# Attention with a two-layer network on one core: each half of the last output block is stored by one transfer with two pieces of 64 rows, from SyncE, in place of two transfers

## The chip, the core and the metric

The kernel runs on one core of one Trainium2 chip. Times are microseconds of device time of that core, from one execution of the whole program. The kernel before takes 636.6 us (median of 3 runs, 635.3 to 640.33). One further execution was profiled: its own time is 637.86 us, and its span, from the first to the last instruction of the profile, is 636.1 us.

## What is computed

Four sequences of 576 tokens go through attention with 8 heads of 64, whose scores get a bias from a small network on the relative position. The result, 2304 tokens by 512, goes through two matrix products with a squared ReLU between them. Everything is float32 for the reader of the output.

```python
def _attn_ref(q, k, v, w1, b1, w2):
    ...
    scores = scale * np.matmul(q, k.transpose(0, 1, 3, 2))
    ...
    scores = scores + bias.transpose(2, 0, 1)[None, :, :, :]
    ...
    return np.matmul(attn, v).astype(np.float32)

def _moe_ref(x, w_in, w_out):
    h = np.maximum(x @ w_in, 0.0)
    return (h * h @ w_out).astype(np.float32)

def reference(**kwargs):
    ...
    x = np.ascontiguousarray(attn_out.transpose(0, 2, 1, 3)).reshape(B * S, H * D)
    return _moe_ref(x=x, **moe_kwargs)
```

## The kernel before

**Tiling.** The four sequences are two pairs p. A sequence has four whole blocks of 128 tokens and a remainder of 64; the block c = 0 holds the remainders of both sequences of a pair, 64 tokens in the lower 64 partitions and 64 in the upper ones. So a pair has five blocks, and `order` lists all ten (k = 0 to 9). For each block and head, `qk`, `softmax_a`, `softmax_b`, `turn` and `pv` do the attention; `norm` and `turn_x` scale and transpose the block's result; then `g1(n)`, `square(n)`, `g2(n)` do the network in eight units of hidden columns each (n = 8 k + u), and `store(k, b)` writes the block to `out`. Float32 operands are split into pairs of float16 tiles, so each product is three matmuls.

**The last block.** The last block, k = 9, is the remainder block of the second pair. For it `g2` is "halved": the 512 output columns are computed as two halves of 256 columns (L865 to L875), each in its own PSUM tile `blk["o", d]`, so that the first half is finished one group of six matmuls ahead of the second. `store` (L882 to L898) then takes the halves d = 0 and d = 1 in turn: one scaling instruction moves a half from PSUM to an SBUF tile `o` of 128 x 256 (ScalarE at L889 for d = 0, VectorE at L887 for d = 1), and two transfers bring it to `out`, one for the 64 rows of each sequence (L895). The two pieces of a half lie 576 rows apart in `out`. SyncE issues three of the four transfers, ScalarE the last (d = 1, bb = 1). All transfers write rows of 256 float32, 1 KB each, at a pitch of 2 KB.

**What sets the order.** `PROGRAM` is one long string of words written by hand; each word takes the generator of that kind one step further (`next(live[word], None)`), so what stands between two `yield`s is recorded at one word. Every engine runs its own instructions in the order in which they were recorded. The word `ou:9.0` is the last block's store; it stands once ahead of the last step of `g2:79` and then at the end of the string. SyncE issues nearly all transfers of the kernel in this order and does no arithmetic; a transfer that waits holds back those behind it. The program ends when the last transfer has landed and all engines have come to the closing branch (L1014).

Of the kernel before, what the change touches and what calls it, by code (L numbers as in the profile page):

```python
# [16 lines left out]
B, H, S, D = 4, 8, 576, 64  # L17
DM, DFF = 512, 2048
# [179 lines left out]
)  # L198


# [1 line left out]
def tile_attention_moe(  # L202
# [11 lines left out]
    nc = tc.nc  # L214
# [55 lines left out]
    def zn(key, i):  # L270
        v = ENG[key]
        return v[min(i, len(v) - 1)]
# [606 lines left out]
    def store(k, b):  # L879
        blk = blks[k]  # L880
        p, c = blk["p"], blk["c"]
        if k == len(order) - 1 and not c:  # L882
            for d in range(2):
                r = slice(256 * d, 256 * d + 256)
                o = r_p.tile([128, 512], F32, tag="r", name="o")
                if d:
                    nc.vector.tensor_scalar(o[:, 0:256], blk["o", d][:, 0:256], blk["os"][:, 0:1], None, op0=ALU.mult)  # L887
                else:
                    nc.scalar.activation(out=o[:, 0:256], in_=blk["o", d][:, 0:256], func=AF.Copy,  # L889
                                         scale=blk["os"][:, 0:1])  # L890
                yield
                for bb in range(2):
                    r0 = (2 * p + bb) * S + 512
                    q = nc.scalar if d and bb else nc.sync
                    q.dma_start(out=out[r0:r0 + 64, r], in_=o[64 * bb:64 * bb + 64, 0:256])  # L895
                    if not d or not bb:
                        yield
            return  # L898
        o = r_p.tile([128, 512], F32, tag="r", name="o")
        if zn("oe", 2 * k + b) == "A":  # L900
            nc.scalar.activation(out=o, in_=blk["o", b], func=AF.Copy, scale=blk["os"][:, b:b + 1])
        else:
            nc.vector.tensor_scalar(o, blk["o", b], blk["os"][:, b:b + 1], None, op0=ALU.mult)
        yield
        if c:
            r0 = (2 * p + b) * S + 128 * (c - 1)
            nc.sync.dma_start(out=out[r0:r0 + 128, :], in_=o)
        else:
            for bb in range(2):
                r0 = (2 * p + bb) * S + 512  # L910
                nc.sync.dma_start(out=out[r0:r0 + 64, :], in_=o[64 * bb:64 * bb + 64, :])
                if bb == 0:
                    yield
# [104 lines left out]
```

## Time and profile before

| | |
|---|---|
| median of 3 runs | 636.6 us |
| the profiled execution's own time | 637.86 us |
| its span | 636.1 us |
| TensorE busy | 597.7 us (94%) |
| VectorE, GpSimd, ScalarE busy | 428.1, 385.4, 366.5 us |
| mean granted TensorE clock | 0.981 of full speed |
| transfers of the last block | 4 of 64 KB, 3 from SyncE and 1 from ScalarE |

TensorE works nearly without a break up to its last matmul; what follows it is a short end piece in which a scaling instruction, the transfers and the closing of the program come one after the other. The change lies wholly in that end piece. In the rows below, times of day are microseconds from the start of the span, SPq and ACTq are SyncE and ScalarE issuing transfers, and "DMA share" is the mean busy share of the 16 DMA engines.

### The profile page before, as it was taken

To read this page: it belongs to the slowest core of one execution; us is meant where nothing else is said; L and a number is where in the kernel's file an instruction comes from. 1 tells how busy PE (TensorE), PEld (TensorE's weight loads), DVE (VectorE), ACT (ScalarE), POOL (GpSimd) and SP (SyncE) were. 2 spreads that over 40 slices of the span, in tenths; PEclk is the share of its full clock that TensorE was granted. 3 is DMA by queue.
4 is the path that set the end of the run, shared out by engine and by line. 5 is a ranking of instruction groups with operands and counts; after the bars stand their busy time and mean duration, and the time that the engine had idled before them with its cause. 6 is when DMAs were issued, how large, how long until landed. Compare 5 with 4: busy or idle time off the path is not lost.

```text
span 636.1 us, 15958 instructions
## 1 busy us (share of the span) xinstructions
PE 597.7 (94%) x6296; PEld 402.7 (63%) x6296; DVE 428.1 (67%) x840; ACT 366.5 (58%) x779; POOL 385.4 (61%) x389
## 2 busy tenths in 40 slices
PE   5658998899999999999999999999999999999997
PEld 2124576475767467667657865767676686577576
DVE  7988999899669796787974663566456463613321
ACT  5559997687777465645567455746636574214020
POOL 5766499989767435866866647555665555523221
PEclk9669999899999999999999999999999999999999
DMA  8999987778979969799789969559955787623000
GB/s 291 325 285 284 286 237 253 244 188 203 191 183 185 220 159 170 184 226 221 177 164 219 165 131 186 139 115 196 186 136 122 158 169 144 140 34 72 18 34 18
DMA packets 204426, 112.19 MB, mean 176 GB/s; under 512 B 166848, under 2 KB 179392, under 8 KB 204352
## 3 DMA queue, kind: packets, MB, share of 16 engines
q1 hardware_dynamic: 204272, 111.12, 75.2%
q8 instruction: 49, 0.80, 0.5%
q14 instruction: 25, 0.20, 0.1%
q10 hardware_dynamic: 80, 0.07, 0.0%
HBM read 55.44 MB, written 15.61 MB: 112 GB/s over the span
## 4 chain that ended last, share of the span: by engine, by line
PE 51%; DMA 5%; DVE 5%; POOL 4%; issue 3%; ACT 2%; SPq 1%; POOLq 0%; DVEq 0%; ACTq 0%
PE hp L837 20%; PE o L872 19%; PE pv L757 5%; PE sc L637 5%; DMA at<-a 3%; DMA xt<-xh 2%; POOL a L712 2%; PE bp L542 1%; DVE s L656 1%; POOL g L857 1%; DVE g L280 1%; ACT s L669 1%; DMA stg<-vd 1%; DVE r L851 1%; ACT a L276 1%
## 5 line engine op out<-in xcount | busy, mean ns | idle before, releaser
L837 PE MATMUL hp<-xt,winH 128*128 128x256 f16 (+1 forms) x1280 | 193.3, 262 | 2.0 <-DVE r L851 1.1
L872 PE MATMUL o<-woutH,g 128*128 128x512 f16 (+1 forms) x608 | 186.4, 369 | 2.2 <-POOL g L857 1.6
L837 PE MATMUL hp<-xt,winL 128*128 128x256 f16 (+1 forms) x640 | 161.7, 262 | 0.0
L857 POOL TENSOR_TENSOR g<-r,g 128x512 f16<-128x512 f32 (+1 forms) x80 | 88.4, 1108 | 88.3 <-DVE g L280 81.5
L872 PEld LDWEIGHTS <-g 128*128 128x128 f16 x912 | 84.3, 98 | 90.5 <-issue 4.5
L712 POOL TENSOR_TENSOR a<-s,a 128x1024 f16<-128x1024 f32 (+1 forms) x64 | 133.1, 2079 | 0.0
L837 PEld LDWEIGHTS <-winH 128*128 128x128 f16 x1280 | 117.8, 98 | 20.6 <-DVE r L851 1.2
L656 DVE CUSTOM_DVE_ANT_0 s<-sc,bt 128x576 f32<-128x576 f32 x144 | 104.6, 749 | 35.7 <-PE sc L637 15.2
L851 DVE TENSOR_TENSOR r<-hp,r 128x512 f32<-128x512 f32 (+1 forms) x80 | 50.7, 634 | 105.6 <-ACT r L849 105.2
L872 PE MATMUL o<-woutL,g 128*128 128x512 f16 (+1 forms) x304 | 112.1, 369 | 0.0
L669 ACT ACTIVATE s<-s,nm 128x576 f32<-128x576 f32 x120 | 92.9, 774 | 6.6 <-ACT nm L667 0.4
L710 POOL TENSOR_TENSOR a<-s,a 128x128 f16<-128x128 f32 (+1 forms) x64 | 30.3, 473 | 105.6 <-ACT a L276 73.7
L849 ACT ACTIVATE r<-hp 128x512 f32<-128x512 f32 (+1 forms) x80 | 43.7, 546 | 85.4 <-PE hp L837 75.2
L757 PE MATMUL pv<-v,at 128*128 128x64 f16 (+5 forms) x2112 | 87.8, 203 | 1.9 <-ACT at L276 1.2
L667 ACT ACTIVATE nm<-mx,esc 128x1 f32<-128x1 f32 x120 | 34.4, 287 | 84.2 <-DVE mx L656 84.0
L276 ACT ACTIVATE a<-s 128x1152 f16<-128x1152 f32 (+1 forms) x64 | 70.3, 1098 | 14.6 <-DMA at<-a 13.5
L837 PEld LDWEIGHTS <-winL 128*128 128x128 f16 x640 | 62.6, 98 | 5.8
L757 PEld LDWEIGHTS <-at 128*128 128x128 f16 (+1 forms) x1792 | 55.0, 100 | 10.4 <-issue 3.6
L477 DVE TENSOR_SCALAR hg<-tab_t 128x464 f32<-128x464 f32 (+17 forms) x88 | 60.9, 723 | 0.7 <-PE bp L542 0.6
L280 DVE TENSOR_SCALAR g<-r 128x512 f16<-128x512 f32 (+1 forms) x64 | 48.0, 754 | 18.4 <-PE o L872 17.4
L637 PE MATMUL sc<-k,q 64*128 64x128 f16 (+1 forms) x768 | 58.2, 284 | 1.3 <-DVE mx L656 1.2
L637 PEld LDWEIGHTS <-q 64*128 64x128 f16 x768 | 39.6, 94 | 28.1 <-issue 19.0
(88 smaller groups left out, 687.1 us busy)
## 6 DMA issues: line engine op xcount, KB each, us to landing
bt<-biasd SPq DMA_DIRECT2D x64, 288.0 KB, 3.5
stg<-w_in SPq DMA_DIRECT2D x16, 512.0 KB, 6.0
stg<-w_out SPq DMA_DIRECT2D x16, 512.0 KB, 5.5
biasd<-be SPq DMA_DIRECT2D x16, 295.5 KB, 6.2
bt<-biasd SPq DMA_DIRECT2D x32, 144.0 KB, 4.7
qst<-qd SPq DMA_DIRECT2D x32, 128.0 KB, 3.3
out<-o SPq DMA_DIRECT2D x16, 256.0 KB, 2.5
v<-vd SPq DMA_DIRECT2D x8, 320.0 KB, 7.0
```

Of the source, the lines that this page charges most:

```text
L276: nc.scalar.activation(out=out, in_=in_, func=AF.Copy, scale=scale)
L280: nc.vector.tensor_scalar(out, in_, scale, None, op0=ALU.mult)
L477: nc.vector.tensor_scalar(ht, src, scl[:, n:n + 1], None, op0=ALU.min)
L637: i = nc.tensor.matmul(out=sc[:, o:o + w], lhsT=qt[r, qz, qs], rhs=kt[r, z, k0:k0 + w], start=(m == 0), stop=(m == 2), tile_position=(64 * ...
L656: nc.vector.tensor_tensor_reduce(s[:, 576 * b:576 * b + 576], sc[:, sb:sb + 576], bt, inv, 3.0e38, ALU.add, ALU.min, mx[:, b:b + 1])
L669: nc.scalar.activation(out=sl, in_=sl, func=AF.Exp, scale=-1.0, bias=mx[:, b:b + 1] if f32 else nm[:, b:b + 1], accum_out=su[:, h, b:b + 1])
L712: eng.tensor_tensor(av[:, :, 640:1152], ev[:, :, 0:512], av[:, :, 0:512], op=ALU.subtract)
L757: nc.tensor.matmul(out=dst, lhsT=lhsT, rhs=rhs, start=b not in [x[1] for x in seq[:j]], stop=b not in [x[1] for x in seq[j + 1:]], tile_po ...
L837: nc.tensor.matmul(out=hp[:, f * T:f * T + T].rearrange("p (b t) -> p b t", b=nb), lhsT=wt[:, k, c0:c0 + 128], rhs=xt[:, 0:nb, z * 4 + k, ...
L851: nc.vector.tensor_tensor(rr, hp[:, 0:2 * T], rr, op=ALU.mult)
L857: eng.tensor_tensor(g[:, 1, 0:2 * T], rr, g[:, 0, 0:2 * T], op=ALU.subtract)
L872: nc.tensor.matmul(out=blk["o", b][:, 0:256] if halved else blk["o", b], lhsT=g[:, z, c0:c0 + 128], rhs=wt[:, 2 * u + f, d], start=(u == 0 ...
```

## The change

In `store`, for the last block, the loop over the two sequences goes. One transfer from SyncE takes the whole tile `o[:, 0:256]` (128 partitions) to a destination that is written out as a pattern of three steps: 2 pieces a whole sequence apart, 64 rows in each, 256 elements in a row. ScalarE issues no transfer any more. The string loses two words, since the store has two steps fewer.

```diff
-    "ou:9.0 ou:9.0 ou:9.0 ou:9.0 ou:9.0 "
+    "ou:9.0 ou:9.0 ou:9.0 "
...
                 yield
-                for bb in range(2):
-                    r0 = (2 * p + bb) * S + 512
-                    q = nc.scalar if d and bb else nc.sync
-                    q.dma_start(out=out[r0:r0 + 64, r], in_=o[64 * bb:64 * bb + 64, 0:256])
-                    if not d or not bb:
-                        yield
+                dst = out[2 * p * S + 512:2 * p * S + 576, r]
+                dst = bass.AP(tensor=dst.tensor, offset=dst.offset, ap=[[S * DM, 2]] + [list(x) for x in dst.ap])
+                nc.sync.dma_start(out=dst, in_=o[:, 0:256])
+                if not d:
+                    yield
             return
```

At the very end of the program the instructions on SyncE are, before (the destination's shape stands behind the names; `o_9543` is the half d = 0, `o_9553` the half d = 1, `DVE_49` and `Activation_49` count finished instructions of VectorE and ScalarE, and the DMAHW names count landed transfers):

```order
L825 DMA_TRANSPOSE xt_9135<-xh_9126 128x8x128 [waits DMAHW3_49,DVE_49]
L907 DMA out<-o_9272 128x512 [waits DMAHW4_49,Activation_49]
L907 DMA out<-o_9356 128x512 [waits DMAHW5_49,Activation_49]
L895 DMA out<-o_9543 64x256 [waits Activation_49]
L895 DMA out<-o_9543 64x256 [waits DMAHW7_49]
L895 DMA out<-o_9553 64x256 [waits DMAHW1_49,DVE_49]
L1014 UNCONDITIONAL_BRANCH
```

And of the changed kernel, on SyncE at the same place (`o_9552` is now the half d = 1; all line numbers behind the edit are one lower):

```order
L825 DMA_TRANSPOSE xt_9135<-xh_9126 128x8x128 [waits DMAHW3_49,DVE_49]
L906 DMA out<-o_9272 128x512 [waits DMAHW4_49,Activation_49]
L906 DMA out<-o_9356 128x512 [waits DMAHW5_49,Activation_49]
L894 DMA out<-o_9543 2x64x256 [waits Activation_49]
L894 DMA out<-o_9552 2x64x256 [waits DMAHW7_49,DVE_49]
L1013 UNCONDITIONAL_BRANCH
```

Three transfers became two; the destination of both begins with a count of 2. The transfer of the second half stands directly behind that of the first and waits for VectorE's scaling and for the transfer of an earlier block. On ScalarE the end of the program before is:

```order
L849 ACTIVATE r_9409<-hp_9366 128x256 [waits DMAHW4_49,PE_49,Activation_49]
L849 ACTIVATE r_9489<-hp_9439 128x256 [waits PE_49,Pool_49]
L849 ACTIVATE r_9507<-hp_9464 128x256 [waits PE_49,Pool_49]
L889 ACTIVATE o_9543<-o0_9275,os_9115 128x256 [waits DMAHW5_49,PE_49,Activation_49]
L895 DMA out<-o_9553 64x256 [waits DVE_49]
L1014 UNCONDITIONAL_BRANCH
```

In the changed kernel the row `L895 DMA` is gone from ScalarE and the other rows stand as they did. On TensorE, VectorE and GpSimd no instruction is added, removed or moved.

## Rows read from the trace of the kernel before

**Rows 1.** Chain that ended last, 600:637 us: start us, us, what (first and last pieces)

```profile
599.11 1.16 POOL g L857
...
623.70 2.68 PE hp L837 x48
626.38 5.25 PE o L872 x48
631.63 0.02 issue
631.66 0.48 DVE o L887
```

**Rows 2.** Timeline, 624:637 us: start us, us, engine line op out<-in xcount [idle before]

```profile
631.05 0.47 ACT L889 ACTIVATE o<-o,os 128x256 f32<-128x256 f32 x1 [4.19 <-PE o L872]
631.35 0.27 PE L872 MATMUL o<-woutH,g 128*128 128x256 f16 x1
631.55 1.79 SPq L895 DMA_DIRECT2D out<-o  x3
631.66 0.48 DVE L887 TENSOR_SCALAR o<-o,os 128x256 f32<-128x256 f32 x1 [3.94 <-PE o L872]
632.18 0.56 ACTq L895 DMA_DIRECT2D out<-o  x1
```

**Rows 3.** Waits of SyncE, 620:637 us: engine line, us in total, times, longest

```profile
SPq L895 <- ACT o L889: 14.0, 1, 14.0
SPq L1014 <- DMA out<-o: 1.4, 1, 1.4
SPq L1014 <- PEq L1014: 0.9, 2, 0.7
```

**Rows 4.** Line 895: ns min/median/max of one issue, first and last start us; landing

```profile
L895 SPq DMA_DIRECT2D out<-o x3: 513/540/585, 631.6 to 632.8; - x3
L895 ACTq DMA_DIRECT2D out<-o x1: 562/562/562, 632.2 to 632.2; - x1
...
DMA to landing us min/median/max: 2.0/2.0/2.3
```

**Rows 5.** DMA queues, 631:637 us: packets, MB, share of 16 engines

```profile
q1 hardware_dynamic: 240, 0.20, 13.3%
q10 hardware_dynamic: 80, 0.07, 4.5%
```

**Rows 6.** Stretches of the end: length, five engines busy (x instructions), clock, DMA share, GB/s

```profile
632.40:632.60 0.20, 0.00 (x0) 0.00 (x0) 0.00 (x0) 0.00 (x0) 0.00 (x0) 1.00 0.00 0
632.60:632.80 0.20, 0.00 (x0) 0.00 (x0) 0.00 (x0) 0.00 (x0) 0.00 (x0) 1.00 0.19 51
632.60:633.20 0.60, 0.00 (x0) 0.00 (x0) 0.00 (x0) 0.00 (x0) 0.00 (x0) 1.00 0.44 109
634.20:634.40 0.20, 0.00 (x0) 0.00 (x0) 0.00 (x0) 0.00 (x0) 0.00 (x0) 1.00 0.63 149
634.40:634.60 0.20, 0.00 (x0) 0.00 (x0) 0.00 (x0) 0.00 (x0) 0.00 (x0) 1.00 0.01 0
```

**Rows 7.** DMA queues and issues, 617.5:620 us, where one whole-block store runs

```profile
q1 hardware_dynamic: 144, 0.26, 27.2%
issues: line engine op xcount, KB each, median us to landing
out<-o SPq DMA_DIRECT2D x1, 256.0 KB, 2.0
```

**Rows 8.** The page's DMA queues over the whole span: packets, MB, share of 16 engines

```profile
q1 hardware_dynamic: 204272, 111.12, 75.2%
```

**Rows 9.** Line 416, loads of 64 x 4 x 64: ns of one issue, landing

```profile
L416 SPq DMA_DIRECT2D qst<-qd x8: 601/613/749, 1.7 to 501.1; - x8
...
DMA to landing us min/median/max: 2.5/3.8/5.0
```

## Prediction

> **What bounds the kernel now.** I read the chain of waits first: from 599 us to the end it is TensorE, with only 1.16 us of GpSimd and then 0.48 us of VectorE that are not matmuls [rows 1]. The change touches no matmul, so the first 631.6 us stay as they are, and all that can move is the end piece from there to 636.1. The timeline gives it step by step [rows 2]. ScalarE scales the first half from 631.05 to 631.52; TensorE ends at 631.62; VectorE scales the second half from 631.66 to 632.14. SyncE issues from 631.55 to 633.34 three transfers one after the other, about 0.54 us each [rows 2, 4]; ScalarE issues the fourth at 632.18. SyncE's last issue starts at 632.8 and lands 2.0 us after its start, at 634.8; ScalarE's lands at 632.18 + 2.3 = 634.5 [rows 4]. So the last to land is the third of SyncE's queue. Behind it SyncE waits at the closing branch, 1.4 us for the transfer and 0.9 for TensorE's queue to close [rows 3], and the span ends.
>
> For the DMA engines the stretches show [rows 6]: nothing before 632.6, first rows on their way in 632.6 to 632.8 (I take 632.7, about 1.15 us after the first issue began at 631.55), and no more data after about 634.4. From the end of the data to the end of the span are 636.1 - 634.4 = 1.7 us, which I keep for all cases: landing, then closing.
>
> **What the change removes.** Two of four issues: 0.54 us on SyncE and 0.56 on ScalarE [rows 4]. With 16 engines at work on each transfer this would be a gain. VectorE is done at 632.14, SyncE's first issue ends at about 632.1, so the second half would be issued at 632.2 in place of 632.8, and its first rows would run at 632.2 + 1.15 = 633.3.
>
> **What it adds.** An issue with three steps in the destination. None to `out` is in the trace; the nearest are the loads with 64 x 4 x 64, 0.613 us against 0.54 [rows 9, 4], so +0.07 us, and nothing below zero since a pattern of more steps has no cheaper row. Only the first of the two would be on the path, and I price it at 0 to 0.1. The second lies beside the first transfer's data. Nothing is queued behind either but the closing branch.
>
> **What it moves: which DMA engines carry the rows.** This is the term that decides. Each transfer of 64 rows shows 80 packets: 64 rows and 16 closing packets, one for each engine; SyncE's three show 240, that is 3 x 80 [rows 5]. A store of 128 rows shows 144 = 128 + 16 [rows 7]. So a transfer whose outermost count is 64 or 128 on both sides is dealt out over all 16 engines in whole rows, 4 or 8 to each. The new transfer has 128 on the side it reads and 2 on the side it writes. The trace has no such transfer, so the cost has two bounds. If the rows are still dealt out over 16 engines, each carries 8. If the work is cut along the outermost count and the cut must fit both sides, only two equal parts are possible: two engines with 64 rows each, and the other 14 idle. I take the second, since what is seen of the dealing is always an equal cut of an outermost count that both sides share, and 2 is all that these two share.
>
> The Trainium skill, page "DMA: Bandwidth & Descriptors", section "Why a DMA increments its semaphore by 16 and not by 1", states this: the engine count is the largest number up to 16 that divides the slowest dimension of both patterns, and a transfer from SyncE or ScalarE uses the lowest-numbered engines. By that rule the count here is 2, and both transfers go to the same two. No run here shows it yet; the trace agrees for 64 and 128 rows (16 closings). At that page's rate of about 27 GiB/s for an engine, 64 KB would take an estimated 2.3 us, and the time by it would be about 639.4 us.
>
> **The price of one row on one engine.** Two rows of the trace bound it. The store of 128 rows of 2 KB keeps the engines busy for 27.2% of 2.5 us x 16 = 10.9 us, or 85 ns for 2 KB [rows 7]; half is 43 ns for 1 KB. The four transfers at the end take (13.3% + 4.5%) x 6 us x 16 = 17.1 us for 256 rows, 67 ns for 1 KB [rows 5]; the first of them alone, 0.44 x 0.6 x 16 = 4.2 us for 64 rows, 66 ns [rows 6]. Is 67 a matter of the short row? If a packet cost f + s per KB, 67 and 85 would give f = 49 ns; but over the whole span 204272 packets of 544 bytes on average took 0.752 x 636.1 x 16 / 204272 = 37 ns each [rows 8], less than f alone. So the 64-row stores are slow for another reason, and they differ from the 2 KB store in that they read 64 partitions with 16 engines, where it reads 128. Two engines that read from 128 partitions crowd each other less than either. I take 46 ns, just above half of the 2 KB row, and keep 67 as the other end.
>
> **The sum.** A transfer is 64 x 46 ns = 2.94 us on its two engines. The second half's rows are ready at 633.3, while the first's run until 632.7 + 2.94 = 635.6; they queue behind them on the same two engines. Data ends at 632.7 + 5.9 = 638.6, and the span at 638.6 + 1.7 = 640.3, which is 4.2 us over 636.1. The profiled execution's 637.86 us would become 642.1; it stood 1.3 us above the median of 636.6, so for the median I expect 636.6 + 4.2 = 640.8 us, 0.66% more. A measurement of this kernel can tell about 1% from no change, so this is a small loss that counts as "within 1%".
>
> **Rivals.**
> Slow rows on two engines (slower by over 1%). The rows cost 67 ns as in the four transfers of before: 64 x 67 ns = 4.3 us a transfer, data until 641.3, span 643.0, +6.9, 643.5 us. For it: it is the price of just these 1 KB rows to just this place in memory [rows 5]. Against it: the 37 ns of the mean packet [rows 8], and that 16 engines no longer share 64 partitions. It decides from +6.4 us on, that is 8.1 us of data, 63 ns a row.
>
> Sixteen engines (a small gain). The pattern is dealt out over all engines: 8 rows each, 8 x 46 ns = 0.37 us; the second half runs from 633.3 to 633.7, span 635.4, -0.7, 635.9 us. For it: every transfer of the trace does so [rows 5, 7]; against it: the common count of 2. The Trainium skill, page "SBUF — State Buffer", section "Can I just issue two DMAs to hit both halves?", speaks for the change: two transfers of 64 partitions each reach only half the ports, one over 128 reaches all. The slow rows at the end (67 ns against 43) agree with it; what it would give here is this rival's time.
>
> Two engines each, but not the same two. The second half runs from 633.3 to 636.2 beside the first: span 637.9, +1.8, 638.4 us. Nothing in the trace tells which engines a short transfer gets.
>
> The change does all it says in either case; what could be empty is its gain, since the issues removed are 0.6 us of the path at most.
>
> **How the numbers follow.** Forecast (two engines, the same two, 46 ns): 0.55, its own range 639.5 to 642. Slow rows: 0.17. Sixteen engines: 0.16. Separate pairs: 0.07. The remaining 0.05 is for a single engine that takes still longer over a row than 67 ns, above 645. The runs of before lie between 635.3 and 640.3, so a median can be off by about 1 us, and the range is widened by that much. From 636.3 to 644.0 it holds nearly all of the forecast (0.53) and of the separate pairs, most of the slow rows (0.14) and a third of the sixteen engines (0.06): 0.80. Slower by over 1% (above 643.0): more than half of the slow rows, the remainder, and a little of the forecast by scatter, 0.18. Faster by over 1%: 0.01, as no case gains more than 0.7 us. Within 1%: 0.81.
>
> **What would show it.** In the changed profile two SyncE issues of about 0.6 us at 631.55 and 632.2, none on ScalarE. The engine count shows in the packets: 128 rows with 2 closings (260 for both) if two engines work, 288 if sixteen do, and in a DMA share near 2/16 = 0.13 from 632.7 to 638.6 in place of 0.6 to 0.9. The landing would be about 4.2 us after its issue for the first and over 6 for the second. If the share stays above 0.5 and ends by 633.9, the forecast is wrong at the dealing; if it lies at 0.13 and ends near 641, the row's price is; if it lies at 0.25 for a while, the pairs are separate. TensorE's rows up to 631.6 should not move.

## The result: 0.66% slower, as two DMA engines out of 16 carry the last block

The changed kernel takes 640.36 us (median of 21 runs, 638.94 to 645.86) against 636.11 us of the kernel before (21 runs, 633.3 to 640.33). The ratio is 1.0066, with a 95% interval of 1.0049 to 1.0083: about 4.2 us more.

From the page of the changed kernel, its span and the busy times of the engines:

```profile
span 638.0 us, 15956 instructions
...
PE 595.2 (93%) x6296; PEld 402.6 (63%) x6296; DVE 427.0 (67%) x840; ACT 366.8 (57%) x779; POOL 385.2 (60%) x389
```

The timeline of its end, from 628 us (start us, us, engine line op out<-in xcount):

```profile
628.59 0.47 ACT L889 ACTIVATE o<-o,os 128x256 f32<-128x256 f32 x1 [4.19 <-PE o L872]
...
628.89 0.27 PE L872 MATMUL o<-woutH,g 128*128 128x256 f16 x1
629.09 1.32 SPq L894 DMA_DIRECT2D out<-o  x2
629.20 0.48 DVE L887 TENSOR_SCALAR o<-o,os 128x256 f32<-128x256 f32 x1 [3.94 <-PE o L872]
```

Against [rows 2] the last matmul ends at 629.16 in place of 631.62. That is scatter of this one execution in the 629 us ahead, where nothing was changed (the runs of before spread over 7 us), and it hides part of the loss when the two spans are compared: 638.0 - 636.1 is only 1.9. So from here on all is read in the **end piece**, from the end of the last matmul to the end of the span: before 636.1 - 631.6 = 4.5 us, now 638.0 - 629.2 = 8.8. The difference of 4.3 us is that of the medians.

Where it lies, the waits of SyncE say (engine line, us in total, times, longest), which answer to [rows 3]:

```profile
SPq L894 <- ACT o L889: 14.0, 1, 14.0
SPq L1013 <- DMA out<-o: 6.2, 2, 3.5
SPq L1013 <- PEq L1013: 0.9, 2, 0.7
```

The closing branch waited 1.4 us for the transfers and now waits 6.2; the 0.9 us behind it is the same. The DMA queues from 626 to 640 us (the digits are the busy share in tenths in 40 slices; below them the GB/s, then packets, MB and share), to be held against [rows 5]:

```profile
DMA  0000000000000111111111111111110000000000
GB/s 0 0 0 0 0 0 0 0 0 0 0 0 18 29 35 32 38 26 41 53 47 47 47 50 50 47 47 50 50 44 0 0 0 0 0 23 0 0 0 0
...
q1 hardware_dynamic: 260, 0.26, 5.9%
```

There are 260 packets: 256 rows and 4 closings, two for each transfer, where before it was 16 for each. And stretches of the changed kernel's end (length, five engines busy, granted clock, DMA share, GB/s), against [rows 6]:

```profile
630.20:630.60 0.40, 0.00 (x0) 0.00 (x0) 0.00 (x0) 0.00 (x0) 0.00 (x0) 1.00 0.11 20
...
631.00:632.00 1.00, 0.00 (x0) 0.00 (x0) 0.00 (x0) 0.00 (x0) 0.00 (x0) 1.00 0.13 35
632.00:633.00 1.00, 0.00 (x0) 0.00 (x0) 0.00 (x0) 0.00 (x0) 0.00 (x0) 1.00 0.14 40
...
633.80:634.80 1.00, 0.00 (x0) 0.00 (x0) 0.00 (x0) 0.00 (x0) 0.00 (x0) 0.50 0.14 49
...
636.40:636.60 0.20, 0.00 (x0) 0.00 (x0) 0.00 (x0) 0.00 (x0) 0.00 (x0) 0.50 0.05 15
636.60:638.00 1.40, 0.00 (x0) 0.00 (x0) 0.00 (x0) 0.00 (x0) 0.00 (x0) 0.50 0.00 0
```

A share of 0.13 is 2 of 16. It stays near that from 630.3 to 636.5, 6.2 us, where the 256 rows of before ran from 632.7 to 634.4, 1.7 us. TensorE has run nothing since 629.2; from 633.8 on its clock is granted at 0.50 of full speed, the lower level of 1.2 GHz, and SyncE's wait for its queue to close is 0.9 us as before.

### The profile page after: what moved, and what is told of

It is laid out like the page before. It is cut to its first block, busy times and chain, and to the rows that moved or that the text cites. A ratio compares the mean times of both kernels' runs of the same rounds, so it can differ in the third digit from the quotient of the medians.

```text
span 638.0 us, 15956 instructions
## 1 busy us (share of the span) xinstructions
PE 595.2 (93%) x6296; PEld 402.6 (63%) x6296; DVE 427.0 (67%) x840; ACT 366.8 (57%) x779; POOL 385.2 (60%) x389
## 4 chain that ended last, share of the span: by engine, by line
PE 56%; DVE 4%; DMA 4%; POOL 3%; issue 2%; SPq 1%; ACT 1%; POOLq 0%; DVEq 0%; ACTq 0%
PE hp L837 23%; PE o L872 21%; PE pv L757 6%; PE sc L637 5%; DMA xt<-xh 2%; PE bp L542 1%; POOL g L857 1%; POOL a L712 1%; DVE s L656 1%; PE sc L623 1%; DMA stg<-vd 1%; DMA at<-a 1%; DVE g L280 1%; SPq L719 1%; POOL v L278 1%
## 5 line engine op out<-in xcount | busy, mean ns | idle before, releaser
L276 ACT ACTIVATE a<-s 128x1152 f16<-128x1152 f32 (+1 forms) x64 | 70.3, 1099 | 16.3 <-DMA at<-a 15.3
```

The source lines that it names most:

```text
L276: nc.scalar.activation(out=out, in_=in_, func=AF.Copy, scale=scale)
```

## Experiments

The theory (A) says: the transfer is dealt over as many DMA engines as the outermost counts of both of its sides share; 128 and 2 share 2, and all such transfers go to the same two engines. The rivals: a transfer to two far pieces or with three steps is slow in itself (B); the price of the rows is that of the short stores of before, 67 ns, on any engine (C); each queue has engines of its own. The runs on the last block stand in one table (e8 is about other transfers and comes last). The end piece comes from one profiled execution of each run, the ratio from timed rounds beside the kernel before. e1, e2 and e3 leave the rows of the last block in another order than the reference, so they are for their times only.

| run | stores of the last block | packets | end of span - end of last matmul = end piece, us | time over before (95%) |
|---|---|---|---|---|
| before | 4 of 64 rows, outermost 64 | 320 | 636.1 - 631.62 = 4.5 | 1 |
| changed | 2 of 2 x 64 rows | 260 | 638.0 - 629.16 = 8.8 | 1.0066 (1.0049 to 1.0083) |
| e1 | 2 of 64 x 2 rows | 288 | 631.9 - 628.01 = 3.9 | 0.999 (0.9971 to 1.0009) |
| e2 | 4 of 2 x 32 rows | 264 | 641.2 - 631.46 = 9.7 | 1.0071 (1.0054 to 1.0087) |
| e3 | 4 of 4 x 16 rows | 272 | 633.9 - 627.12 = 6.8 | 1.0007 (0.9989 to 1.0026) |
| e4 | as changed, second from ScalarE | 260 | 639.3 - 630.47 = 8.8 | 1.0071 (1.0048 to 1.0093) |
| e5 | as before, 2 from each queue | 320 | 632.3 - 628.15 = 4.15 | 0.9998 (0.9979 to 1.0017) |
| e6 | 2 of 64 x 2 rows, tokens interleaved | 288 | 636.1 - 631.57 = 4.5 | 1.0009 (0.9988 to 1.0029) |
| e7 | first half as changed, second as before | 290 | 635.5 - 629.01 = 6.5 | not timed, one execution |

**e1: the two outer steps exchanged.**

```diff
-dst = bass.AP(..., ap=[[S * DM, 2]] + [list(x) for x in dst.ap])
+dst = bass.AP(..., ap=[list(dst.ap[0]), [S * DM, 2], list(dst.ap[1])])
```

> The changed kernel with the first two steps of the destination exchanged: 64 rows outermost, 2 pieces inside, in place of 2 and 64. The same bytes, still one transfer of 128 partitions for each half, still two far pieces, still three steps; the rows of the two sequences come out interleaved, so this run is for its time only. All is measured in the end piece, from the end of the last matmul to the end of the span: 4.5 us in the kernel before (636.1 - 631.6), 8.9 us in the changed kernel (638.0 - 629.1).
> Theory A (the transfer is dealt over as many engines as the outermost counts of both sides share): 64 and 128 share 16, so 16 engines, 288 packets, 8 rows an engine at 46 ns = 0.4 us a transfer; first rows 1.3 us after the first issue, the second transfer's 0.7 later, data over 2.5 us after the last matmul, end piece 3.9 us, about 0.6 below the kernel before and 5 below the changed one; time about 0.999 of before, 635.5.
> Theory B (a transfer from one tile to two far pieces, or with three steps, is slow in itself): 260 to 288 packets, end piece 8 to 9 us, time 1.0066 of before.
> Theory C (the rows cost 67 ns on 16 engines whatever they read): 288 packets, end piece 4.1 us, and 256 rows take 17 us of engine time; by A they take 12.

The timeline of its end, and the DMA queues from 627 us to the end of the window at 632:

```profile
627.74 0.27 PE L872 MATMUL o<-woutH,g 128*128 128x256 f16 x1
627.95 1.29 SPq L894 DMA_DIRECT2D out<-o  x2
```

```profile
DMA  0000000000000000018992059940000000000000
GB/s 0 0 0 0 0 0 0 0 0 0 0 0 0 0 0 0 0 41 287 352 295 74 0 213 344 352 140 0 0 0 0 0 0 0 0 0 0 0 0 0
...
q1 hardware_dynamic: 288, 0.26, 15.3%
```

288 = 256 + 2 x 16: all engines work again, in two short bursts with a share of 0.9, one for each half. The end piece is 631.9 - 628.0 = 3.9 us, 4.9 less than in the changed kernel and 0.6 less than before, with the same bytes, the same one transfer for each half, the same three steps and the same two far pieces. So B falls. So does C: 15.3% of 5 us x 16 is 12.2 us, or 48 ns for each of 256 rows, where the stores of 64 rows took 67 [rows 5]. The 0.6 us under the kernel before holds the issues saved and the cheaper rows together; no run separates the two, and it is one execution (e6, with the same stores, did not repeat it). The Trainium skill, page "SBUF — State Buffer", section "Can I just issue two DMAs to hit both halves?", holds here as far as it goes: one transfer over 128 partitions moved its rows faster than two over 64. The order of the steps on the other side cost 4.9 us, eight times what that gained.

**e2: outermost count 2 without far pieces.** Four transfers as before, each to the even and the odd rows of one sequence.

```diff
-q.dma_start(out=out[r0:r0 + 64, r], in_=o[64 * bb:64 * bb + 64, 0:256])
+dst = bass.AP(..., ap=[[DM, 2], [2 * DM, 32], [1, 256]])
+q.dma_start(out=dst, in_=o[64 * bb:64 * bb + 64, 0:256])
```

> The kernel before, with its four transfers of 64 rows from SyncE (three) and ScalarE (one), each with its destination written as 2 x 32 rows: the outermost count is 2, the pieces lie next to each other (even and odd rows of the 64 of one sequence; the rows come out permuted, so this run is for its time only).
> Theory A (engines by the common outermost count): 2 engines for each of four transfers, 264 packets (256 rows, 8 closings), the same two engines for all and so 128 rows an engine in sequence, 5.9 us of data at 46 ns: end piece 8.6 to 8.9 us like the changed kernel, time 1.006 of before.
> Theory B (far pieces out of one tile are slow): no far pieces here, end piece 4.5 us as before, 320 packets.
> If the transfer from ScalarE's queue ran on other engines than those from SyncE's, data would be over a quarter earlier: end piece about 7.2.

DMA queues from 629 us on (packets, MB, share), and the stretch in which data runs:

```profile
q1 hardware_dynamic: 198, 0.20, 5.1%
q10 hardware_dynamic: 66, 0.07, 1.8%
```

```profile
632.60:639.60 7.00, 0.00 (x0) 0.00 (x0) 0.00 (x0) 0.00 (x0) 0.00 (x0) 0.59 0.13 37
```

198 = 3 x (64 + 2) from SyncE and 66 from ScalarE: two engines for each transfer though nothing lies far apart. The end piece is 641.2 - 631.5 = 9.7 us, 0.8 us or more over the 8.6 to 8.9 of the expectation. The share is 0.13 for all of 7 us, so the four transfers do not run on engines of their own beside each other.

**e3: outermost count 4.** The same with `[[DM, 4], [4 * DM, 16], [1, 256]]`.

> As the run before it, with each destination written as 4 x 16 rows, outermost count 4 (rows permuted, for its time only).
> Theory A: 4 engines for each transfer, 272 packets (256 rows, 16 closings), 16 rows an engine and transfer, four transfers in sequence on the same four engines = 64 rows x 46 ns = 2.9 us of data from 1.1 us after the first issue: end piece 1.1 + 2.9 + 1.6 = 5.6 us, 1.1 above before; time 1.002 of before, which the rounds may not resolve; the profile must.
> Theory B: 320 packets, end piece 4.5 us. A DMA share of 0.25 while data runs (4 of 16) is A's mark.

DMA queues from 627 to 634 us, and the stretch in which data runs:

```profile
q1 hardware_dynamic: 204, 0.20, 9.5%
q10 hardware_dynamic: 68, 0.07, 2.7%
```

```profile
628.20:632.20 4.00, 0.00 (x0) 0.00 (x0) 0.00 (x0) 0.00 (x0) 0.00 (x0) 0.73 0.21 66
```

204 = 3 x (64 + 4): four engines each, at a share of 0.21 to 0.25. The number of engines follows the outermost count: 2, 4, and 16 for a count of 64. The end piece is 633.9 - 627.1 = 6.8 us, where 5.6 was expected; data runs for nearly 4 us and not 2.9. In e2 the excess is about the same 1 us. The price of a row does not explain it; more on it stands in the last section. By its end piece the run should take 2.3 us more than before (1.0036); the rounds gave 1.0007 with an upper end of 1.0026, so they do not bear that number out, and with runs that scatter over several us in the stretch ahead I trust the profile for the mechanism only.

**e4: the second half from ScalarE's queue.**

```diff
-nc.sync.dma_start(out=dst, in_=o[:, 0:256])
+(nc.scalar if d else nc.sync).dma_start(out=dst, in_=o[:, 0:256])
```

> The changed kernel, the second half's transfer issued by ScalarE in place of SyncE.
> Theory A with the same two engines for every queue: the two transfers share the two engines, row by row or one behind the other; 260 packets, DMA share 0.13 throughout, data for 5.9 us, end piece 8.8 to 8.9 us as in the changed kernel, time 1.006 of before.
> Rival (each queue has its own two engines, or SyncE's queue alone is what holds the second transfer back): the second half runs beside the first, DMA share 0.25 for about 2.5 us, data over 3.6 us after the first row, end piece 6.4 us, time 1.003 of before.

DMA queues from 629 us on (slices, packets), the stretch in which data runs, and the issues of line 894:

```profile
DMA  0000000010111111111111111110000000000000
...
q1 hardware_dynamic: 130, 0.13, 3.5%
q10 hardware_dynamic: 130, 0.13, 2.8%
```

```profile
631.60:637.90 6.30, 0.00 (x0) 0.00 (x0) 0.00 (x0) 0.00 (x0) 0.00 (x0) 0.57 0.13 42
```

```profile
L894 SPq DMA_DIRECT2D out<-o x1: 680/680/680, 630.4 to 630.4; - x1
L894 ACTq DMA_DIRECT2D out<-o x1: 1144/1144/1144, 631.0 to 631.0; - x1
```

130 packets from each queue and still a share of 0.13, so both queues use the same two engines. The end piece is 639.3 - 630.5 = 8.8 us, the ratio 1.0071: no gain, and the rival with engines for each queue (6.4 us) falls. The Trainium skill, page "DMA: Bandwidth & Descriptors", states both halves of this, the count in the section "Why a DMA increments its semaphore by 16 and not by 1" (2 engines for 2, 4 for 4, by these packets) and, in the section "Issuing engines are not separate DMA queues", that a second issuing engine buys no second set of engines; these runs agree with both.

**e7: only the first half in the new form.**

```diff
+if not d:
+    ... one transfer with two pieces, as in the changed kernel
+    continue
 for bb in range(2):
     ... two transfers of 64 rows, as before
```

> Only the first half leaves by one transfer with two pieces; the second half by two transfers of 64 rows as before (SyncE and ScalarE).
> Theory A: the first half's 128 rows on two engines for 3.0 to 3.4 us; the second half's 128 rows are dealt over 16 engines, but the 16 of them that fall to those two engines queue behind: data for 3.5 to 3.8 us, 290 packets, end piece 6.3 to 6.5 us, nearly half of the loss (2.2 of 4.3 us less).
> Rival (the second transfer's share of the loss does not come from queueing on the same engines but from its own slowness): end piece over 7 or the second half landing after 16 engines' time, 4.5 us.
> It also tells whether the first 64 rows of an engine (3.4 us in the changed kernel, 64 x 46 would be 2.9) are slowed by the second transfer of the same form: with it gone they should take 3.0 by that reading, 3.4 if the pace at the start belongs to the transfer itself.

The end piece is 635.5 - 629.0 = 6.5 us, as A has it. The DMA rows of its end, from 627 to 642 us in slices of 0.375 us, and the issues show that the second half's transfers pay too (the last number is the landing in us after the issue):

```profile
DMA  0000000001111586110000000000000000000000
GB/s 0 0 0 0 0 0 0 0 16 38 33 38 27 74 161 208 46 46 11 0 0 0 0 22 0 0 0 0 0 0 0 0 0 0 0 0 0 0 0 0
...
q1 hardware_dynamic: 210, 0.20, 4.2%
q10 hardware_dynamic: 80, 0.07, 3.2%
...
out<-o ACTq DMA_DIRECT2D x1, 64.0 KB, 4.5
out<-o SPq DMA_DIRECT2D x1, 64.0 KB, 4.5
```

These two run over 16 engines (80 packets each) and landed in 2.0 to 2.3 us in the kernel before [rows 4]. Here it is 4.5 us, and the trace shows two reasons. The first is that on all engines their rows begin late: the GB/s rise above those of two engines only from 631.9 on, 2.2 to 2.3 us after the issues at 629.6 and 629.7, where the kernel before had 1.15. What holds them is not shown. The second is the queueing of A. The trace keeps the moment at which each engine counted its part of a transfer as landed: of the sixteen counts of either transfer fourteen came by 633.1 and 633.3, the last two by 634.1 and 634.25, about 0.9 us later. On these two engines their rows stand behind those of the first half. A transfer is done when its slowest engine is.

**e5: two issues from each queue, with 16 engines.**

```diff
-q = nc.scalar if d and bb else nc.sync
+q = nc.scalar if bb else nc.sync
```

> The kernel before, four transfers of 64 rows with all 16 engines, but of each half the first sequence's rows are issued by SyncE and the second's by ScalarE (before: three by SyncE, one by ScalarE).
> Theory A (with 16 engines the end piece hangs on the last issue, at 632.8 of SyncE's queue): each queue issues two, the last issue starts when VectorE is done, 0.6 us earlier; the rows, 67 ns each on 16 engines, are over about 0.5 us earlier: end piece 4.0 us against 4.5 in the kernel before; time 0.999 of before, less than the rounds tell apart.
> Rival (the data of 256 rows at 67 ns on 16 engines is the limit, 1.1 us in all, or the two queues hold each other up): end piece 4.5 us or more.

The end piece is 632.3 - 628.15 = 4.15 us (expected 4.0), 0.35 less than before, in one execution. The time, 0.9998 (0.9979 to 1.0017), cannot tell that from nothing.

**e6: a complete version with the rows outermost.** The squared activations of the last block are written with the tokens of the two sequences alternating, so that row r of both sequences stands in neighbouring partitions.

```diff
+rv = rr.rearrange("p (f r b) -> p f b r", f=2, b=2)
+hv = hv.rearrange("p (f b r) -> p f b r", f=2, b=2)
-nc.scalar.activation(out=rr, in_=hp[:, 0:2 * T], ...)
+nc.scalar.activation(out=rv, in_=hv, ...)
...
+nc.sync.dma_start(out=os2[bb:128:2, 0:1], in_=blk["os"][64 * bb:64 * bb + 64, 0:1])
...
-dst = bass.AP(..., ap=[[S * DM, 2]] + [list(x) for x in dst.ap])
+dst = bass.AP(..., ap=[list(dst.ap[0]), [S * DM, 2], list(dst.ap[1])])
```

> A complete version of the run with rows outermost: the squared activations of the last block are written so that its 128 tokens stand interleaved (row 0 of both sequences, row 1 of both, ...), the scale of each token is brought into the same order by two small transfers some 50 us before the end, and each half leaves by one transfer with 64 rows outermost and the 2 pieces inside.
> Theory A: 16 engines, 288 packets in the last two stores, end piece 3.9 us as in the run with rows outermost, 0.6 below the kernel before, if the strided writes of ScalarE and VectorE in the last block (8 units, 0.38 and 0.42 us each now) do not delay TensorE. Time 0.999 of before (635.5), 0.993 of the changed kernel.
> Rival: the strided writes take over 0.7 us each and TensorE waits for them in the last block: the stretch from 611 us to the last matmul grows by 1 us or more and the gain is gone, time 1.000 to 1.005 of before.

288 packets again, and TensorE was not delayed: from the last GpSimd piece of the chain (599.06) to VectorE's scaling (631.61) are 32.55 us, as in [rows 1]. But the end piece is 636.1 - 631.6 = 4.5 us and not 3.9. Stretches of its end:

```profile
633.40:633.80 0.40, 0.00 (x0) 0.00 (x0) 0.00 (x0) 0.00 (x0) 0.00 (x0) 1.00 0.76 274
633.80:634.20 0.40, 0.00 (x0) 0.00 (x0) 0.00 (x0) 0.00 (x0) 0.00 (x0) 1.00 0.21 62
634.20:634.60 0.40, 0.00 (x0) 0.00 (x0) 0.00 (x0) 0.00 (x0) 0.00 (x0) 0.53 0.08 13
634.60:635.00 0.40, 0.00 (x0) 0.00 (x0) 0.00 (x0) 0.00 (x0) 0.00 (x0) 0.50 0.00 0
```

Most rows are through by 634.0, but about one engine (0.08 of 16) goes on after that. In the trace's counts fifteen engines had landed their part of the second transfer by 634.4 and the last one at 635.1, 0.7 us later; in e1 all sixteen counts of a transfer lie within 0.2 us. One profiled execution does not say whether it belongs to the version or to that execution. The time, 1.0009 (0.9988 to 1.0029), is that of the kernel before. So no version here is shown to beat the kernel before; e6 and e5 beat the changed one.

**e8: the same form on loads in mid-kernel.** The bias loads of the two remainder blocks have the same shape of problem: 64 rows for the lower and 64 for the upper partitions.

```diff
-BONE = False
+BONE = True
...
 src = bass.AP(tensor=src.tensor, offset=src.offset, ap=[[0, 2]] + [list(x) for x in src.ap])
 nc.sync.dma_start(out=t, in_=src)
```

> The same form on loads in mid-kernel: the kernel before, with the bias loads of the two remainder blocks (16 pairs of loads of 64 rows of 2304 bytes) each made one load whose source has 2 pieces of 64 rows (the same rows twice) outermost.
> Theory A: 2 engines for each, 64 rows of 92 ns = 5.9 us of data on each, one load behind the other on the same two engines, so landing 8 us or more after the issue (4.7 median now), and all transfers over 16 engines wait for those two. The first eight are read 3 us apart from 41 to 65 us, twice as fast as the two engines can bring them: VectorE waits there, 8 x 5.9 = 47 us from 29 us on, the last at 78 in place of 65; with other work in between I expect 1.01 to 1.03 of before.
> Rival (loads in mid-kernel have enough cover): landing longer but the time within 0.3% of before.

The time is 697.82 us, 1.0978 of before (1.0952 to 1.1004): ten per cent, far above the 1 to 3 that I expected. DMA from 60 to 90 us of this run, and its first 100 us as one stretch:

```profile
DMA  1118969111121689821112511117985931111397
GB/s 63 52 49 339 200 229 400 46 49 49 49 74 52 123 310 358 333 96 49 49 49 85 157 49 49 52 57 200 319 268 112 341 122 49 49 52 44 82 189 174
```

```profile
0.00:100.00 100.00, 51.50 (x363) 23.38 (x364) 54.99 (x114) 43.20 (x89) 44.28 (x57) 0.74 0.61 200
```

In nearly half of the slices only two engines work (share 0.1, about 49 GB/s). The same 100 us of the kernel before had a share of 0.94 and 285 GB/s. That transfers over all engines are held back with them is seen in VectorE's waits of these 100 us (us in total, times, longest):

```profile
DVE ci L362 <- DMA stg<-w_out: 20.2, 4, 10.6
DVE ci L362 <- DMA stg<-w_in: 13.3, 3, 6.2
DVE s L656 <- DMA bt<-biasd: 5.3, 1, 5.3
```

In the kernel before these three were 1.4, 0.9 and 1.5 us, 35 us less in sum. So VectorE waited mostly for the weight loads, whose form was not changed, and little for the bias loads themselves. The writes to `biasd`, from 128 partitions, landed 14.1 us after their issue (median of 28 to 100 us; 6.6 in 28 to 66 us before). SyncE was held as well, so a transfer can be late by its issue or by its rows, and no run separates the two for the weights. This is the longest issue in its timeline; the same one took 0.53 us before:

```profile
34.03 8.21 SPq L349 DMA_DIRECT2D stg<-w_out  x1
```

My estimate had priced the loads' own rows against the time in which they are read, and left out that those two engines were already busy with their sixteenth of everything else. A reckoning made after the run fits better: each load puts 64 rows on either of two engines where two loads of 64 had put 8, so 56 x 92 ns = 5.2 us more for each load, 41 us for the eight of a block (92 ns is the estimate of the expectation for 2304 bytes; the 49 GB/s of two engines give 94). In the first block, where the DMA engines were full, VectorE's eight reads now span 41.1 to 98.1 us in place of 41.0 to 65.0, 33 us more. The whole span grew by 58.5 (694.6 - 636.1). VectorE's reads of the bias stay 33 us behind those of before up to 519 us of that kernel's time, and the rest is lost from there to its 566 us, at the second remainder block. That the second block loses by the same mechanism was not tested by itself, nor how much of the loss belongs to TensorE's clock (0.74 granted in the first 100 us, 0.90 before).

## Why the prediction was right

**The dealing.** This was the term that decided, and it held: 260 packets, a share of 0.13. In the prediction it rested on an inference, that the dealing is an equal cut of an outermost count that both sides share. e1, e2 and e3 show that it is: 16, 2 and 4 engines for outermost counts of 64, 2 and 4, with three steps in all of them, with and without far pieces. In e8 the count of 2 stood on the side that is read. Only powers of two were tried.

**The same two engines.** e4 and e7 show it: no gain from the other queue, and the last two of sixteen counts come 0.9 us after the others.

**The price of a row.** I took 46 ns and 5.9 us of data; it was 6.2 us, 48 ns a row. That this came so near is in part luck, since the mean has two paces in it that I did not forecast: 20 to 40 GB/s up to 633 us, and 49 GB/s from 633.8 on, which is 2 x 1024 bytes in 42 ns. The first transfer's rows took 3.4 us on their two engines and the second's 2.7, where I had 2.94 for each. The other end, 67 ns, was the price of 16 engines that read 64 partitions; one transfer of 128 partitions on 16 engines paid 48 (e1).

**The issue.** 0.55 and 0.66 us (line 894 of the changed kernel, below) against the 0.54 before and the 0.61 taken from the nearest row:

```profile
L894 SPq DMA_DIRECT2D out<-o x2: 554/609/664, 629.1 to 629.9; - x2
```

First rows came 1.2 us after the first issue began (I had 1.15, and 0 to 0.1 for the third step).

**What stands behind the data.** 638.0 - 636.5 = 1.5 us, not 1.7.

**The sum.** The end piece grew by 4.3 us, forecast 4.2: 0.3 more of data, up to 0.1 more ahead of it, 0.2 less behind. The ratio I gave was 640.8 / 636.6 = 1.0066, and that was measured; the 0.4 us between 640.8 and 640.36 is the base, whose median fell from 636.6 to 636.11 with more runs. The loss lies within 1%, as forecast; 21 runs of either kernel tell so small a loss from none (1.0049 at the least).

**The rivals.** Sixteen engines, which I had put at 0.7 us, was worth 0.6 in e1's execution, but only with the rows outermost, and nothing in e6's. Slow rows and separate pairs did not occur. For the landing I gave 4.2 us after the issue and over 6 as marks. The views have no landing for these two transfers, but the trace's counts have: two engines for each, the last at 634.1 and at 636.85 us. That is 5.0 and 7.0 us after the issues at 629.1 and 629.9, so the first was later than I said, by the slow pace at the start.

Of the expectations, e2, e3 and e6 came out 0.6 to 1.2 us longer in the end piece than I had said, and one failed clearly, e8: the direction was right and the size short by a factor of three or more, for the reason told there.

## What to carry to other kernels

Before two transfers are joined into one, look at the outermost count on both sides: if the joined pattern begins with a 2, two DMA engines do the work of 16, and the packets of the profile tell it (rows plus the closings of each engine). The issue saved is half a microsecond; the price is the rows of 14 idle engines, 4.3 us here, and in mid-kernel it is paid by the other transfers too, which have rows on the same two (e8, ten per cent). Put the larger count outermost, or leave the two transfers.

## What I had not expected of the hardware

ScalarE's issue grew longer when few engines took its rows. It lasted 0.56 us with 16 engines [rows 4] and up to 0.77 in e5, 1.14 in e4, and in e2 and e3 (line 897, ns):

```profile
L897 ACTq DMA_DIRECT2D out<-o x1: 1397/1397/1397, 632.0 to 632.0; - x1
```

```profile
L897 ACTq DMA_DIRECT2D out<-o x1: 1159/1159/1159, 627.7 to 627.7; - x1
```

SyncE's issues in e2, e3 and e4, on as few engines, lasted 0.51 to 0.69 us against 0.51 to 0.59 before, so few engines alone do not make an issue long; what does in ScalarE's case is not shown. In e8, where the two engines were behind with their rows, an issue on SyncE lasted 8.2 us.

Rows on few engines also start slowly. In the changed kernel single rows of 67 to 249 ns stand among rows of 46 ns up to 632.4 us, and none after it; this is the slow pace of the first transfer, and such rows may be the extra 1 us of e2 and e3. Two causes can be set aside by e7, which had them too. A second transfer of this form is not needed: e7 has only one, and its rows took 3.3 us on their two engines, as long as the 3.4 of the changed kernel. And the later issues do not make them by running at the same time: in e7 the last issue ended at 630.2, and the rows stayed slow until 631.9. What makes them slow stays open.
